# One tile for both heads' first 64 tokens in half of the attention units

## The chip, the cores and the metric

The kernel runs on one core of a Trainium2 chip. The metric is device time of one execution in microseconds, and of the kernel before three executions were timed. TensorE is called PE below, VectorE DVE, ScalarE ACT, GpSimd POOL, and the queue of SyncE that issues most DMAs SP.

## What is computed

Four batches of 8 heads, 576 tokens of 64 elements: causal attention plus a linear memory, mixed by a gate per head; then two feed-forward layers over the 2304 tokens (512 to 2048 to 512), all in float32.

```python
scores = np.where(causal, -1e9, scale * q @ k.T); scores -= scores.max(-1, keepdims=True)
a = np.exp(scores); a /= a.sum(-1, keepdims=True) + 1e-09
q_p = phi(q)                       # exp(min(q, 0)) + max(q, 0)
mem_out = (q_p @ M_prev) / (q_p @ z_prev + 1e-06)
x = g * mem_out + (1 - g) * (a @ v)
h = x @ w_in1;  x = (s * relu(h) ** 2 + b) @ w_out1
h = x @ w_in2;  x = (h * tanh(softplus(h))) @ w_out2
```

## The kernel before

**Attention units.** Function `pair` (L469) makes the steps of one unit: a batch, a pair of heads and a group of query tiles. Each head's 576 queries are padded with 64 rows of zeros in front, which gives five tiles of 128. A *leading* unit takes tiles 0 to 2, that is 320 tokens a head and 64 rows of padding in tile 0; a *trailing* unit takes tiles 3 and 4. There are 16 of each kind, 4 in each batch.

In a leading unit each head has its own tile `Pt` for t = 0, 1, 2, six in all, of 128 rows and 64 + (64 + 128 t) columns: the memory part and the keys up to the diagonal. The steps are: loads of q rows with z (`qn`, L514), of transposed q and k (`qk`, L521) and of M with v (`vx`, L656); phi(q), its product with z and the sums (L535 to L541) on POOL, ACT and DVE; six pairs of score matmuls (L571), the heads of a pair on the upper and lower 64 rows of PE; on DVE a minimum over `mask - scores` that leaves the masked scores in `Pt` (L581); the memory part scaled by `nm` on POOL (L592); the exponential on ACT with its row sum (L589); gate and reciprocal of the sums (L533, L610); the scaling by `rs` on POOL (L607, for batches 1 to 3); transposes on PE, twelve in a leading unit, eighteen in a trailing one (L630); copies out of PSUM on ACT (L635); the product with M and v (L652), for one block of keys after the other, both heads into one bank; a copy (L666) and a store to `x_d` (L668).

**Order of the work.** A planner (`Plan`, L193) writes the order of all engines' instructions down before the program is built. It plays the steps through with a cost, a priority and buffers for each, and what it gives is fixed: every engine takes its instructions in that order. Attention units have the lower number (50 + 7 per unit in batches 1 to 3, L1252) and go ahead of the first feed-forward layer (from 500, `RANK1`), whose matmuls (L881 into the hidden layer, L957 out of it) fill PE while attention waits for other engines. The rings of buffers are short: one of `qn`, `qk`, `vx` at first, two once the weights of layer 1 are converted (L1262), two of `PT`, `xs`, `ex` and of each `Pt`. Stores of the weights' sums and halves for the second layer (L825, L866, L868) go through SP at a late priority, between the loads of attention. At about 312 us attention ends, at about 485 us layer 2 begins (L1112 to L1188), which lasts to the end.

Of the kernel before, what the change touches and what calls it, by code (L numbers as in the profile page):

```python
# [9 lines left out]
F32 = mybir.dt.float32  # L10
F32R = mybir.dt.float32r
BF16 = mybir.dt.bfloat16
I32 = mybir.dt.int32
U32 = mybir.dt.uint32
AF = mybir.ActivationFunctionType
ALU = mybir.AluOpType
# [3 lines left out]
P = 128  # L20
MASKED = -1.0e30
HUGE = 3.0e38
TRUNC = -0.5 + 2.0 ** -13 - 2.0 ** -15
PE, ACT, DVE, POOL, DMA = range(5)
# [29 lines left out]
def act_us(n, extra=0):  # L54
    return 0.094 + 0.00083 * n + 0.093 * extra


def dve_us(n, fast=False):
    return 0.068 + (0.00052 if fast else 0.00104) * n


def pool_us(n):
    return 0.3 + 0.0013 * n
# [6 lines left out]
def two(s):  # L70

    s.two = True
    return s
# [119 lines left out]
class Plan:  # L193
# [29 lines left out]
    def add(self, engine, us, prio, f, r=(), w=(), after=(), keep=(), share=1.0):  # L223


        bufs = list({id(b): b for b in (*r, *w, *keep) if b.ring is not None}.values())
        new = [b for b in bufs if b.maker is None]
        waits = {id(s): s for b in r for s in b.writers}
        waits.update((id(s), s) for s in after)
        s = Step(engine, us, prio, f, list(waits.values()), bufs, new)  # L230
        s.share = share
        s.left = len(waits)
        for x in waits.values():
            x.next.append(s)
        for b in bufs:
            b.users += 1
            if b.maker is None:
                b.maker = s
            elif id(b.maker) not in waits:
                b.maker.next_start.append(s)  # L240
                s.left += 1
        for b in w:
            b.writers.append(s)
        self.steps.append(s)
        return s
# [114 lines left out]
def attention_then_two_ffn(ctx: ExitStack, tc: tile.TileContext, qk, qz, vm, beta,  # L360
# [3 lines left out]
    nc = tc.nc  # L364
    B, H = qk.shape[:2]
    NQ, D = qz.shape[3] - 1, qz.shape[4]
    SP = NQ * P
    S = SP - D
# [16 lines left out]
    SCALE = 1.0 / float(D) ** 0.5  # L385
    TA, TB = groups_all = tuple(range(3)), tuple(range(3, NQ))
    NONE = 5
    plan = Plan()
    add = plan.add
# [6 lines left out]
    ident = const.tile([P, P], F32, name="ident")  # L396
    make_identity(nc, ident)
    mask = const.tile([P, SP], BF16, name="mask")
# [3 lines left out]
    igate = const.tile([P, 2, H], F32, name="igate")  # L402
    sb = const.tile([P, 2], F32, name="sb")

    x_d = dram.tile([P, NCC, NT], F32, name="x_d")
# [9 lines left out]
    x_in = {(b, g): Buf() for b in range(B) for g in range(2)}  # L415
# [21 lines left out]
    small, att = ExitStack(), ExitStack()  # L437
    m1s = small.enter_context(tc.tile_pool(name="m1s", bufs=1))
    at = att.enter_context(tc.tile_pool(name="at", bufs=1, side="right"))
    m1t, m2a, m2c = [], [], []  # L440

    R = {}
# [22 lines left out]
    attention_steps = []  # L465
# [3 lines left out]
    def pair(b, p, prio, g, place=None, apart=False):  # L469
# [4 lines left out]
        def add(engine, us, f, r=(), w=(), keep=(), share=1.0):  # L474
            attention_steps.append(plan.add(engine, us, prio, f, r, w, keep=keep, share=share))
            return attention_steps[-1]
# [190 lines left out]
        c0 = b * S + q0  # L667
        add(DMA, 0.7, lambda: nc.sync.dma_start(x_d[:, p, c0:c0 + m], xs.t[:, :m]), [xs], [x_in[b, groups_all.index(g)]])  # L668


    W = {}

# [584 lines left out]
    n = len(plan.steps)  # L1257
# [3 lines left out]
    for x, a in zip(("qk", "qn", "vx"), (0, 832, 1344)):  # L1261
        R[x].homes(stage, [a], conversion_left)  # L1262
    for b, p, g, prio in halves_[H:]:
        pair(b, p, prio, g)
    R["c1"] = Ring("c1").homes(stage, [2048 + 256 * i for i in range(4)], conversion_left).more(m1s, 1, conversion_left)
    c1_steps = {"in": {r: [] for r in range(NR)}, "out": {r: [] for r in range(NR)}}
    for r in range(NR):
# [23 lines left out]
    order1, n = [], 0  # L1291
    for i in range(len(seq)):
        order1.append((i, True))
        for k in range(n, len(seq)):
# [3 lines left out]
            n = k + 1  # L1298
# [35 lines left out]
    n = len(plan.steps)  # L1334
# [26 lines left out]
    n = len(plan.steps)  # L1361
# [76 lines left out]
```

## Time and profile before

| | |
|---|---|
| median of 3 runs | 957.14 us (956.62 to 957.4) |
| the profiled execution | 956.4 us, of which its span 954.6 us |
| busy: PE, DVE, ACT, POOL | 98%, 81%, 67%, 23% of the span |
| mean granted PE clock | 0.999 |
| chain that ended last, by engine | PE 79%, DVE 4%, ACT 2%, DMA 1% |

The span runs from the first to the last instruction. Busy time of PE is that of matmuls in flight, so that short waits between matmuls don't show in it; the chain of waits gives starts, and from them the pace.

### The profile page before, as it was taken

To read this page: it belongs to the slowest core of one execution; us is meant where nothing else is said; L and a number is where in the kernel's file an instruction comes from. 1 tells how busy PE (TensorE), PEld (TensorE's weight loads), DVE (VectorE), ACT (ScalarE), POOL (GpSimd) and SP (SyncE) were. 2 spreads that over 40 slices of the span, in tenths; PEclk is the share of its full clock that TensorE was granted. 3 is DMA by queue.
4 is the path that set the end of the run, shared out by engine and by line. 5 is a ranking of instruction groups with operands and counts; after the bars stand their busy time and mean duration, and the time that the engine had idled before them with its cause. 6 is when DMAs were issued, how large, how long until landed. Compare 5 with 4: busy or idle time off the path is not lost.

```text
span 954.6 us, 19318 instructions
## 1 busy us (share of the span) xinstructions
PE 937.3 (98%) x6594; PEld 862.0 (90%) x6594; DVE 776.0 (81%) x1886; ACT 641.5 (67%) x1393; POOL 220.7 (23%) x377
## 2 busy tenths in 40 slices
PE   7899999999999999999999999999999999999998
PEld 6677788878788999888899999999999999999998
DVE  6999989899978787568658998889957799577874
ACT  6899878777777476889757865557634476344652
POOL 4635445577663000000023400000000000000000
PEclk9999999999999999999999999999999999999999
DMA  9976757999996789988885658885786655775545
GB/s 236 311 201 176 235 162 224 266 267 265 283 257 198 221 282 308 291 301 274 291 289 165 206 184 266 303 278 177 234 285 218 209 163 191 259 226 199 170 139 178
DMA packets 148339, 224.11 MB, mean 235 GB/s; under 512 B 15120, under 2 KB 122640, under 8 KB 141328
## 3 DMA queue, kind: packets, MB, share of 16 engines
q1 hardware_dynamic: 141408, 174.63, 59.4%
q0 software_dynamic: 6688, 48.24, 15.3%
q8 instruction: 52, 0.85, 0.4%
q14 instruction: 47, 0.39, 0.1%
q10 hardware_dynamic: 144, 0.00, 0.0%
HBM read 159.39 MB, written 63.44 MB: 233 GB/s over the span
## 4 chain that ended last, share of the span: by engine, by line
PE 79%; DVE 4%; ACT 2%; DMA 1%; issue 1%; POOL 0%; DVEq 0%; POOLq 0%
PE bank L1112 20%; PE bank L1185 19%; PE bank L881 12%; PE bank L957 12%; PE bank L1188 5%; PE bank L652 4%; PE bank L630 4%; PE bank L571 3%; DMA stage<-wi_sums_d 1%; DVE S L740 1%; DMA qn<-in_qz 0%; DVE g L1118 0%; DVE woh L740 0%; POOL Pt L607 0%; DVE g L1150 0%
## 5 line engine op out<-in xcount | busy, mean ns | idle before, releaser
L1112 PE MATMUL bank<-wi,woh 128*128 128x384 f32 x477 | 112.5, 334 | 0.0
L1112 PE MATMUL bank<-wi,wol 128*128 128x384 f32 x483 | 105.9, 335 | 0.8 <-DVE wil L1118 0.6
L1185 PE MATMUL bank<-wol,S 128*128 128x256 f32 x756 | 102.3, 283 | 0.0
L1185 PE MATMUL bank<-woh,S 128*128 128x256 f32 x756 | 101.9, 283 | 0.0
L1185 PEld LDWEIGHTS bank<-wol,S 128*128 128x128 f32 x756 | 96.2, 192 | 0.0
L1185 PEld LDWEIGHTS bank<-woh,S 128*128 128x128 f32 x756 | 95.9, 192 | 0.0
L1112 PEld LDWEIGHTS bank<-wi,wol 128*128 128x128 f32 x483 | 85.6, 188 | 1.6 <-DVE wil L1118 0.9
L1112 PEld LDWEIGHTS bank<-wi,woh 128*128 128x128 f32 x477 | 85.2, 188 | 0.4
L589 ACT ACTIVATE Pt<-Pt,mx 128x64 f32<-128x64 f32 (+4 forms) x152 | 82.6, 564 | 1.8 <-DVE mx L581 1.8
L635 ACT COPY PT<-bank 128x384 f32<-128x384 f32 (+2 forms) x160 | 68.2, 491 | 22.4 <-PE bank L630 15.0
L607 POOL TENSOR_SCALAR Pt<-Pt,rs 128x448 f32<-128x448 f32 (+3 forms) x100 | 65.7, 676 | 39.2 <-DVE rs L610 26.8
L592 POOL TENSOR_SCALAR Pt<-ex,nm 128x64 f32<-128x64 f32 x152 | 60.2, 419 | 63.1 <-DVE nm L541 35.4
L630 PE MATMUL bank<-ident,Pt 128*128 128x128 f32 x444 | 62.5, 275 | 6.1 <-DVE Pt L607 1.7
L630 PEld LDWEIGHTS bank<-ident,Pt 128*128 128x128 f32 x444 | 49.5, 140 | 11.2 <-issue 3.4
L581 DVE CUSTOM_DVE_ANT_0 Pt<-bank,mask 128x64 f32<-128x64 f32 (+3 forms) x152 | 50.5, 373 | 8.0 <-PE bank L571 5.7
L739 ACT CAST woh<-stage 128x1024 fp32r<-128x1024 f32 (+2 forms) x42 | 37.2, 885 | 27.4 <-PE bank L1112 17.9
L740 DVE TENSOR_TENSOR woh<-stage,woh 128x1024 fp32r<-128x1024 f32 (+2 forms) x42 | 42.7, 1018 | 13.8 <-ACT woh L739 13.7
L1125 POOL TENSOR_SCALAR woh<-woh,sb 128x384 f32<-128x384 f32 (+1 forms) x6 | 5.5, 916 | 183.3 <-ACT woh L1124 183.3
L739 ACT CAST S<-g 128x384 fp32r<-128x384 f32 x56 | 28.7, 513 | 27.2 <-PE bank L1185 19.2
L1092 POOL DMA_DIRECT2D woh<-wo_split_d x13 | 6.9, 530 | 156.2 <-DVE g L1150 76.4
L881 PE MATMUL bank<-xh,wi 128*128 128x256 f32 x256 | 42.5, 292 | 0.0
L957 PE MATMUL bank<-gl,woh 128*128 128x256 f32 x256 | 41.5, 288 | 0.0
(331 smaller groups left out, 2491.1 us busy)
## 6 DMA issues: line engine op xcount, KB each, us to landing
woh<-wo_split_d POOLq DMA_DIRECT2D x13, 1024.0 KB, 5.6
wol<-wi_split_d POOLq DMA_DIRECT2D x12, 1024.0 KB, 5.2
wol<-wo_split_d POOLq DMA_DIRECT2D x11, 1024.0 KB, 5.2
stage<-in_w_in SPq DMA_DIRECT2D x21, 512.0 KB, 5.6
stage<-in_w_out SPq DMA_DIRECT2D x19, 512.0 KB, 4.7
stage<-wi_d SPq DMA_DIRECT2D x24, 384.0 KB, 5.1
stage<-wo_d SPq DMA_DIRECT2D x18, 512.0 KB, 3.7
wo_split_d<-high SPq DMA_DIRECT2D x32, 256.0 KB, 4.6
```

Of the source, the lines that this page charges most:

```text
L581: nc.vector.tensor_tensor_reduce(at_t(i, t, D + lo, D + hi), x.t[:, a:a + hi - lo], mask[:, SP - w + lo:SP - w + hi], -SCALE, mx.t[:, i, t ...
L589: nc.scalar.activation(at_t(i, t, D, w + D), at_t(i, t, D, w + D), AF.Exp, bias=mx.t[:, i, t + k:t + k + 1], scale=-1.0, accum_out=rs.t[:, ...
L592: add(POOL, 0.33, lambda i=i, t=t: nc.gpsimd.tensor_scalar(at_t(i, t, 0, D), ex.t[:, i, t - lo_t, :], nm.t[:, i, t - lo_t:t - lo_t + 1], 1 ...
L607: (nc.vector if e == DVE else nc.gpsimd).tensor_scalar(x, x, r, *((None, ALU.mult) if e == DVE else (1.0, ALU.mult, ALU.mult)))
L630: nc.tensor.transpose(ps.t[:, x, :], at_t(i, t, c * P, (c + 1) * P), ident)
L635: (nc.vector.tensor_copy if dve else nc.scalar.copy)(PT[i].t[:, x:x + n], ps.t[:, :n])
L739: lambda: (nc.scalar.copy if e == ACT else nc.vector.tensor_copy)(t[0](0), src()), r, [t[2], half], after)
L740: lo = two(add(DVE, dve_us(n), prio, lambda: nc.vector.tensor_tensor(t[0](1), src(), t[0](0).bitcast(F32), op=ALU.subtract), [*r, half], [ ...
L881: nc.tensor.matmul(ph, w_at(nm, r, cc)[:, o:o + P], x_at(x, cc), start=(begin and part == 0 and cc == 0), stop=(part == 2 and cc == NCC - ...
L957: nc.tensor.matmul(acc[ec // per].t[:, (ec % per) * n:(ec % per + 1) * n], w_at(nm, fc // FPR, fc % FPR)[:, ec * P:(ec + 1) * P], t(x)[:, ...
L1112: nc.tensor.matmul(ps.t[:, :H2], w[i // 4].t[:, j, kk, at_], x[kk].t[:, k], start=begin and part == kk == 0, stop=part == 2 and kk == 1, s ...
L1185: nc.tensor.matmul(acc[t].t[:, :DH], s.t[:, j, t * P:(t + 1) * P], x.t[:, k, q % 4], start=q == part == 0, stop=q == NQ2 - 1 and part == 2)
```

## The change

Leading units of batches 1 to 3 (twelve of sixteen) are made by a new function `leading` in place of `pair`. Both heads' 64 tokens of tile 0 go into one tile from the minimum on, head 0 on rows 0 to 63 and head 1 on rows 64 to 127, so that a unit has five tiles instead of six. The score matmuls stay six, in pairs of equal width, with q taken at columns that put the tokens on the right rows. The gates are laid out for five tiles once at the start (`gates`), with the triangle for 64 tokens (`step_`). The load of q rows falls into four DMAs, the product with z into two instructions, and the product with M and v into four pairs of matmuls instead of three.

```diff
+    gates = at.tile([P, 2, H // 2, 5], F32, name="gates")
+    nc.vector.tensor_copy(gates[:, :, :, 1:].rearrange("p k a (h t) -> p (k a) h t", t=2),
+                          igate.rearrange("p k (a h) -> p (k a) h", h=2).unsqueeze(3).to_broadcast([P, H, 2, 2]))
+    step_ = at.tile([P, D], BF16, name="step")
+    for i in range(2):
+        x = slice(D * i, D * i + D)
+        nc.vector.tensor_copy(gates[x, :, :, 0], igate[x, :, i::2])
+        nc.gpsimd.tensor_copy(step_[x], mask[x, SP - P + D * i:SP - P + D * i + D])
...
+    def leading(b, p, prio):
...
+        n_q, n_k, n_s = 320, 384, 5
+        widths = 64, 192, 320, 192, 320
...
+        add(DMA, 0.5, lambda: nc.sync.dma_start(zq(4, 4).rearrange("p (h t) d -> p h t d", t=2), qz[b, hs, :, 2:4].rearrange("h p a d -> p h a d")), w=[q_in])
+        for i in range(2):
+            add(DMA, 0.15, lambda i=i: nc.sync.dma_start(q_in.t[rows(i), 2 * D:4 * D].rearrange("p (s d) -> p s d", d=D), qz[b, 2 * p + i, D:, 0:2]), w=[q_in])
+        add(DMA, 0.25, lambda: nc.sync.dma_start(zq(0, 2), qz[b, hs, :, 0].rearrange("h p d -> p h d")), w=[q_in])
...
+            def weigh(a=a, n=n):
+                x, y, z = zq(3 + a, n), ex.t[:, a:a + n], zq(2, 1)
+                if a:
+                    x, y = (u.rearrange("p (h t) d -> p h t d", t=2) for u in (x, y))
+                    z = zq(0, 2).unsqueeze(2).to_broadcast([P, 2, 2, D])
+                nc.vector.tensor_tensor(x, y, z, op=ALU.mult)
+
+            two(add(DVE, dve_us(n * D), weigh, [ex, q_in], [q_in]))
...
+        where = [(0, 0, 0), (0, 0, D), (1, 0, 0), (0, 1, D), (1, 1, 0)]
+        for x, us, mine in ((0, 256, (0, 1)), (1, 320, (2,))):
+            def mm(x=x, mine=mine):
+                for t in mine:
+                    for i in range(2):
+                        q0 = P * t if t else D - D * i
+                        o, w = (D if t == 1 else 0), widths[t]
+                        nc.tensor.matmul(sc[x][i].t[:, o:o + w], qk_in.t[rows(i), q0:q0 + P], qk_in.t[rows(i), n_k:n_k + w], start=True, stop=True)
+
+            add(PE, 0.03 + us * 0.00167, mm, [qk_in], sc[x], [*(Pt if x == 0 else ()), mx, rs], 1.0)
...
+        for s in (0, 1, 3, 2, 4):
+            w, (x, k, a) = widths[s], where[s]
+
+            if s == 0:
+                for i in range(2):
+                    add(DVE, 0.14 + 0.00105 * w, lambda i=i: nc.vector.tensor_tensor_reduce(
+                        Pt[0].t[rows(i), D:P], sc[0][i].t[rows(i), :D], step_[rows(i)], -SCALE, HUGE, ALU.add, ALU.min, mx.t[rows(i), 0:1]),
+                        [sc[0][i]], [Pt_in[0], mx_in[0]], [Pt[0], mx])
+            else:
...
+        for x, o, blocks in ((0, 0, [(0, 0), (1, 0), (1, 1)]), (1, 0, [(3, 0), (3, 1)]),
+                             (0, 3, [(2, c) for c in range(3)]), (1, 2, [(4, c) for c in range(3)])):
...
+            for c, k in ((0, 0), (0, 1), (1, 1), (2, 1)):
+                for i in range(2):
+                    y = pv.t[rows(i)]
+                    if k == 0:
+                        dest, src = y[:, :D], PT[0].t[:, 0, rows(i)]
+                    elif c < 2:
+                        dest, src = y[:, D:n_q].rearrange("p (t q) -> p t q", t=2), PT[i].t[:, 1 - i + c:4 - i + c:2]
+                    else:
+                        dest, src = y[:, 192:n_q], PT[i].t[:, 5 - i]
+                    nc.tensor.matmul(dest, v_in.t.rearrange("p (h t d) -> p h t d", h=2, d=D)[:, i, c], src,
+                                     start=k == 0, stop=k == 0 or c == 2, skip_group_check=k > 0)
...
     for b, p, g, prio in halves_[H:]:
-        pair(b, p, prio, g)
+        if g == TA:
+            leading(b, p, prio)
+        else:
+            pair(b, p, prio, g)
```

In the built programs PE's last 3133 instructions, those of layer 2, stand in the same order before and after. Up to there the planner moves much. In the order of PE before, the last product of attention stands behind 896 of the 1920 matmuls of layer 1; in that of the change it stands behind 740. Between the scores of one leading unit and those of the next, in the last five intervals before, stand 36, 52, 48, 44 and 44 matmuls of layer 1; in the last six of the change 28, 28, 28, 28, 28 and 32. Score and product matmuls use half of PE's array each; the places where a full-array matmul follows one of them number 40 before and 38 after. From the load of q rows of one leading unit to that of the next, SP has 117 issues in the last five intervals of the change.

PE, the transposes of one leading unit, before (L630 is the transpose, L881 and L957 are matmuls of layer 1):

```order
L630 MATMUL bank_120<-ident,Pt_0_2354 128x128
L630 MATMUL bank_120<-ident,Pt_0_2356 128x128 x2
L881 MATMUL bank_119<-xh_1625,wih_0_1713 128x256 x4
L630 MATMUL bank_124<-ident,Pt_1_2355 128x128
L630 MATMUL bank_124<-ident,Pt_1_2357 128x128 x2
L630 MATMUL bank_126<-ident,Pt_0_2358 128x128 x3
L881 MATMUL bank_119<-xh_1625,wil_0_1722 128x256 x4
L630 MATMUL bank_125<-ident,Pt_1_2359 128x128 x3
```

And in the change, late in attention (L778 is the new transpose, L1090 is what L957 was):

```order
L778 MATMUL bank_125<-ident,Pt_0_3282 128x128
L778 MATMUL bank_125<-ident,Pt_0_3283 128x128 x2
L778 MATMUL bank_123<-ident,Pt_1_3285 128x128 x2
L1090 MATMUL bank_121<-gh_2834,woh_0_2011 128x256 x2
L1090 MATMUL bank_122<-gh_2834,woh_0_2011 128x256 x2
L778 MATMUL bank_126<-ident,Pt_0_3284 128x128 x3
L1090 MATMUL bank_121<-gh_2834,wol_0_2025 128x256 x2
L1090 MATMUL bank_122<-gh_2834,wol_0_2025 128x256 x2
L778 MATMUL bank_120<-ident,Pt_1_3286 128x128 x3
```

One transpose is gone, the groups are 3, 2, 3 and 3 instead of four of 3, and layer 1's matmuls still stand between the groups.

PE, the product with M and v of one leading unit, before and then in the change (64 is the output's rows of a head, the second number its columns):

```order
L652 MATMUL bank_125<-PT_2568,vx_2400 64x384
L652 MATMUL bank_125<-PT_2581,vx_2400 64x384
L652 MATMUL bank_125<-PT_2568,vx_2400 64x256
L652 MATMUL bank_125<-PT_2581,vx_2400 64x256
L652 MATMUL bank_125<-PT_2568,vx_2400 64x128
L652 MATMUL bank_125<-PT_2581,vx_2400 64x128
```

```order
L795 MATMUL bank_120<-PT_3446,vx_3329 64x64 x2
L795 MATMUL bank_120<-PT_3446,vx_3329 64x256
L795 MATMUL bank_120<-PT_3452,vx_3329 64x256
L795 MATMUL bank_120<-PT_3446,vx_3329 64x256
L795 MATMUL bank_120<-PT_3452,vx_3329 64x256
L795 MATMUL bank_120<-PT_3446,vx_3329 64x128
L795 MATMUL bank_120<-PT_3452,vx_3329 64x128
```

The first pair of 384 columns has become one of 64 and one of 256.

SP, the loads of the first leading unit of batch 1, before and then in the change (L702 and L835 load weights):

```order
L702 DMA stage<-in_w_out 128x1024
L656 DMA wil_0_689<-in_vm 128x2x320
L514 DMA qn_775<-in_qz 128x2x256
L521 DMA qk_796<-in_qk 64x2x384 x2
L656 DMA vx_814<-in_vm 128x2x192
```

```order
L664 DMA wil_0_696<-in_vm 128x2x320
L699 DMA qn_782<-in_qz 128x2x128
L701 DMA qn_782<-in_qz 64x128 x2
L702 DMA qn_782<-in_qz 128x2x64
L704 DMA qk_813<-in_qk 64x2x384 x2
L798 DMA vx_833<-in_vm 128x2x192
```

One issue has become four, so that the loads of `qk` and `vx` stand three issues later.

## Rows read from the trace of the kernel before

**Rows 1.** The page: span, and busy time of each engine.

```profile
span 954.6 us, 19318 instructions
...
PE 937.3 (98%) x6594; PEld 862.0 (90%) x6594; DVE 776.0 (81%) x1886; ACT 641.5 (67%) x1393; POOL 220.7 (23%) x377
```

**Rows 2.** Busy time by stretch: PE, PEld, DVE, ACT, POOL, PE clock, DMA share, GB/s.

```profile
200.00:220.00 20.00, 20.00 (x171) 16.61 (x169) 18.48 (x62) 16.37 (x47) 16.48 (x28) 1.00 0.91 257
...
500.00:520.00 20.00, 19.18 (x110) 18.54 (x109) 17.33 (x33) 15.71 (x29) 8.19 (x8) 1.00 0.52 153
540.00:560.00 20.00, 19.16 (x109) 18.55 (x108) 20.00 (x36) 15.02 (x28) 1.88 (x1) 1.00 0.37 124
```

**Rows 3.** The chain of waits, 20 to 320 us: start, length, what.

```profile
204.96 1.29 PE bank L571 x12
206.25 1.45 PE bank L652 x12
207.69 0.67 PE bank L881 x4
208.37 1.96 PE bank L630 x18
210.80 2.03 PE bank L571 x12
212.84 2.10 PE bank L652 x20
214.93 0.67 PE bank L881 x4
215.60 0.48 PE bank L957 x4
...
219.78 1.29 PE bank L571 x12
```

**Rows 4.** Waits of PE, 60 to 320 us: in total, times, longest.

```profile
PE bank L630 <- POOL Pt L607: 1.7, 2, 1.3
PE bank L630 <- ACT PT L635: 0.8, 1, 0.8
PE bank L630 <- DVE nm L533: 0.4, 1, 0.4
```

**Rows 5.** Groups by line and shape, 130 to 310 us: busy us, mean ns, idle before.

```profile
L592 POOL TENSOR_SCALAR Pt<-ex,nm 128x64 f32<-128x64 f32 x100 | 36.7, 390 | 35.2 <-DVE nm L541 20.3 <-PE bank L571 5.9 <-DVE nm L533 3.9
...
L607 POOL TENSOR_SCALAR Pt<-Pt,rs 128x64 f32<-128x64 f32 x20 | 9.7, 500 | 18.0 <-DVE rs L610 14.2 <-ACT Pt L589 2.8 <-ACT xs L666 1.0
...
L581 DVE CUSTOM_DVE_ANT_0 Pt<-bank,mask 128x64 f32<-128x64 f32 x38 | 7.5, 217 | 3.3 <-PE bank L571 3.1 <-POOL Pt L592 0.2
...
L589 ACT ACTIVATE Pt<-Pt,mx 128x64 f32<-128x64 f32 x20 | 7.2, 382 | 0.0
...
L538 DVE TENSOR_TENSOR stage<-ex,stage 128x384 f32<-128x384 f32 x8 | 4.4, 551 | 0.1
```

**Rows 6.** DVE in order of time at the start: start, length, what, idle before.

```profile
7.08 0.17 DVE L430 TENSOR_SCALAR igate<-igate 128x16 f32<-128x16 f32 x1 [0.28 <-ACT igate L429]
8.18 0.69 DVE L717 SCALAR_TENSOR_TENSOR stage<-stage 128x512 int32<-128x512 int32 x1 [0.93 <-ACT stage L713]
```

**Rows 7.** SP issuing DMAs in order of time: start, length, what, count.

```profile
197.08 0.44 SPq L514 DMA_DIRECT2D stage<-in_qz  x1
...
198.12 0.46 SPq L517 DMA_DIRECT2D qn<-in_qz  x1
...
209.66 1.39 SPq L521 DMA_DIRECT2D qk<-in_qk  x2
...
212.28 0.38 SPq L514 DMA_DIRECT2D stage<-in_qz  x1
```

**Rows 8.** DMA issues: KB each, median us from issue to landing.

```profile
qk<-in_qk SPq DMA_DIRECT2D x24, 192.0 KB, 4.0
...
stage<-in_qz SPq DMA_DIRECT2D x8, 256.0 KB, 4.4
```

More of the change, by code (lines that the diff above doesn't have):

```diff
@@ L668, in pair, with add, rows, zq @@
         add(DMA, 0.7, lambda: nc.sync.dma_start(x_d[:, p, c0:c0 + m], xs.t[:, :m]), [xs], [x_in[b, groups_all.index(g)]])
+    def leading(b, p, prio):
+        def add(engine, us, f, r=(), w=(), keep=(), share=1.0):
+            attention_steps.append(plan.add(engine, us, prio, f, r, w, keep=keep, share=share))
+            return attention_steps[-1]
+        hs = slice(2 * p, 2 * p + 2)
+        n_q, n_k, n_s = 320, 384, 5
+        widths = 64, 192, 320, 192, 320
+        qk_in, q_in, v_in = Buf(R["qk"], [P, 2 * n_k]), Buf(R["qn"], [P, 8 * D]), Buf(R["vx"], [P, 6 * D])
+        def rows(i):
+            return slice(D * i, D * i + D)
+        def zq(a, n):
+            return q_in.t[:, a * D:(a + n) * D].rearrange("p (s d) -> p s d", d=D)
+        def q_all():
+            return zq(3, 5)
+        add(DMA, 0.5, lambda: nc.sync.dma_start(zq(4, 4).rearrange("p (h t) d -> p h t d", t=2), qz[b, hs, :, 2:4].rearrange("h p a d -> p h a d")), w=[q_in])
[3 more added lines that the diff above has]
+        for i in range(2):
+            add(DMA, 0.0009 * 2 * n_k, lambda i=i: nc.sync.dma_start(
+                qk_in.t[rows(i)].rearrange("p (a n) -> p a n", a=2),
+                qk[b, 2 * p + i, rows(i)].rearrange("p (a n) -> p a n", a=2)[:, :, :n_k]), w=[qk_in])
+        ex = Buf(R["ex"], [P, n_s, D])
+        nm, mx, rs = (Buf(R[x], [P, 16]) for x in ("nm", "mx", "rs"))
+        n_e = n_s * D
+        def gate(x, k, eps):
+            nc.vector.scalar_tensor_tensor(x, x, eps, gates[:, k, p], op0=ALU.add, op1=ALU.mult)
+        add(POOL, 0.3 + 0.0032 * n_e, lambda: nc.gpsimd.tensor_scalar_min(ex.t, q_all(), 0.0), [q_in], [ex])
+        add(ACT, act_us(n_e), lambda: nc.scalar.activation(ex.t, ex.t, AF.Exp), [ex], [ex])
+        two(add(DVE, dve_us(n_e), lambda: nc.vector.scalar_tensor_tensor(ex.t, q_all(), 0.0, ex.t, op0=ALU.max, op1=ALU.add), [ex, q_in], [ex]))
+        for a, n in ((0, 1), (1, 4)):
+            def weigh(a=a, n=n):
[5 more added lines that the diff above has]
+            two(add(DVE, dve_us(n * D), weigh, [ex, q_in], [q_in]))
+        add(DVE, dve_us(n_e), lambda: nc.vector.tensor_reduce(nm.t[:, :n_s], q_all(), axis=mybir.AxisListType.X, op=ALU.add), [q_in], [nm])
+        add(DVE, 0.15, lambda: gate(nm.t[:, :n_s], 0, 1e-6), [nm], [nm])
+        add(DVE, 0.09, lambda: nc.vector.reciprocal(nm.t[:, :n_s], nm.t[:, :n_s]), [nm], [nm])
+        Pt = [Buf(R["Pt0"], [P, P]), *(Buf(R[f"Pt{t}"], [P, P * (t + 1)]) for _ in range(2) for t in (1, 2))]
+        Pt_in, mx_in, rs_in = ([Buf() for _ in widths] for _ in range(3))
+        sc = [[Buf(R["a"], [P, 512]) for _ in range(2)] for _ in range(2)]
+        where = [(0, 0, 0), (0, 0, D), (1, 0, 0), (0, 1, D), (1, 1, 0)]
[7 more added lines that the diff above has]
+            add(PE, 0.03 + us * 0.00167, mm, [qk_in], sc[x], [*(Pt if x == 0 else ()), mx, rs], 1.0)
+            attention_steps[-1].mode = 1
+        for s in (0, 1, 3, 2, 4):
[6 more added lines that the diff above has]
+            else:
+                add(DVE, 0.14 + 0.00105 * w, lambda s=s, w=w, x=x, k=k, a=a: nc.vector.tensor_tensor_reduce(
+                    Pt[s].t[:, D:D + w], sc[x][k].t[:, a:a + w], mask[:, SP - w:], -SCALE, HUGE, ALU.add, ALU.min, mx.t[:, s:s + 1]),
+                    [sc[x][k]], [Pt_in[s], mx_in[s]], [Pt[s], mx])
+            add(POOL, 0.33, lambda s=s: nc.gpsimd.tensor_scalar(Pt[s].t[:, :D], ex.t[:, s], nm.t[:, s:s + 1], 1.0, op0=ALU.mult, op1=ALU.mult),
+                [ex, nm], [Pt_in[s]], [Pt[s]])
+            add(ACT, 0.28 + 0.00083 * w, lambda s=s, w=w: nc.scalar.activation(
+                Pt[s].t[:, D:D + w], Pt[s].t[:, D:D + w], AF.Exp, bias=mx.t[:, s:s + 1], scale=-1.0, accum_out=rs.t[:, s:s + 1]),
+                [Pt_in[s], mx_in[s]], [Pt_in[s], rs_in[s]], [Pt[s], mx, rs])
+        gated, done = Buf(), Buf()
+        add(DVE, 0.15, lambda: gate(rs.t[:, :n_s], 1, 1e-9), rs_in, [gated], [rs])
+        add(DVE, 0.09, lambda: nc.vector.reciprocal(rs.t[:, :n_s], rs.t[:, :n_s]), [gated], [done], [rs])
+        for s in (0, 1, 3, 2, 4):
+            w = widths[s]
+            add(POOL, pool_us(w), lambda s=s, w=w: nc.gpsimd.tensor_scalar(
+                Pt[s].t[:, D:D + w], Pt[s].t[:, D:D + w], rs.t[:, s:s + 1], 1.0, ALU.mult, ALU.mult), [done, Pt_in[s]], [Pt_in[s]], [Pt[s], rs])
+        PT = [Buf(R["PT"], [P, 9, P]) for _ in range(2)]
+        for x, o, blocks in ((0, 0, [(0, 0), (1, 0), (1, 1)]), (1, 0, [(3, 0), (3, 1)]),
+                             (0, 3, [(2, c) for c in range(3)]), (1, 2, [(4, c) for c in range(3)])):
+            ps, n = Buf(R["a"], [P, 4, P]), len(blocks)
+            def turn(ps=ps, blocks=blocks):
+                for y, (s, c) in enumerate(blocks):
+                    nc.tensor.transpose(ps.t[:, y], Pt[s].t[:, c * P:c * P + P], ident)
+            add(PE, 0.01 + 0.109 * n, turn, [Pt_in[s] for s in sorted({s for s, _ in blocks})], [ps], [PT[x], *(Pt[s] for s, _ in blocks)])
+            add(ACT, act_us(n * P) - 0.04, lambda x=x, o=o, n=n, ps=ps: nc.scalar.copy(PT[x].t[:, o:o + n], ps.t[:, :n]), [ps], [PT[x]])
+        pv, xs = Buf(R["a"], [P, 512]), Buf(R["xs"], [P, 320])
+        def mm():
+            for c, k in ((0, 0), (0, 1), (1, 1), (2, 1)):
+                for i in range(2):
+                    y = pv.t[rows(i)]
[7 more added lines that the diff above has]
+                                     start=k == 0, stop=k == 0 or c == 2, skip_group_check=k > 0)
+        add(DMA, 0.75, lambda: nc.sync.dma_start(v_in.t.rearrange("p (h t d) -> p h t d", h=2, d=D), vm[b, hs, :, :3].rearrange("h p a d -> p h a d")), w=[v_in])
+        add(PE, 0.04 + 704 * 0.00167, mm, PT + [v_in], [pv])
+        attention_steps[-1].mode = 2
+        add(ACT, act_us(n_q) - 0.04, lambda: nc.scalar.copy(xs.t, pv.t[:, :n_q]), [pv], [xs])
+        add(DMA, 0.7, lambda: nc.sync.dma_start(x_d[:, p, b * S:b * S + n_q], xs.t), [xs], [x_in[b, 0]])
```

## Prediction

> **What bounds the kernel now.** I read the page first: PE is busy for 937.3 of 954.6 us, and the next engine, DVE, for 776.0 [rows 1]. A mean over stages with different limits is no proof, so I read the busy time by stretch. While attention and layer 1 share the engines, at 200 to 220 us, PE is busy for all of 20.00 us, DVE for 18.48, ACT for 16.37 and POOL for 16.48 [rows 2]. Then the chain of waits, because it says what ends last there: from 204.96 us on it is PE alone, scores, product, layer 1, transposes, scores, each starting where the one before ends [rows 3]. So in this stretch a microsecond of PE work is a microsecond of time, and work of DVE, ACT or POOL costs nothing as long as PE finds its data ready. Last the waits of PE: from 60 to 320 us they come to 1.7 + 0.8 + 0.4 = 2.9 us, all ahead of transposes [rows 4]. At the start of layer 2, around 510 and 550 us, PE lacks 20.00 - 19.18 and 20.00 - 19.16, together 1.66 us, beside a DVE that is busy for 20.00 [rows 2]. I leave these as they are: PE's order is the same there, and so is the work on the other engines.
>
> **The sum, on PE.** Twelve units change.
>
> *Transposes.* Eighteen take 1.96 us [rows 3], 0.109 us each. One a unit goes: -0.109.
>
> *Scores.* The same six matmuls, with the same widths: 0.
>
> *Product with M and v.* A leading unit streams 384 + 256 + 128 = 768 columns a head in 1.45 us; a trailing one 4 x 256 + 128 = 1152 in 2.10 [rows 3]. The difference gives 0.65 / 384 = 1.69 ns a column, with 1.45 - 768 x 1.69 ns = 0.15 us beside. Now 64 + 256 + 256 + 128 = 704 columns: -64 x 1.69 ns = -0.108. Against that stand two more instructions, a pair with only 64 columns. The trace of before has no such product, so I bound it. Below: nothing, if it costs its columns alone, as the slope between the two units says of wider ones. Above: what 64-column matmuls cost in the scores. Those stream 64 + 192 + 320 = 576 columns in 1.29 us and 64 + 448 + 512 = 1024 in 2.03 [rows 3], which is 1.65 ns a column and 0.34 us beside, 0.19 more than the product has. I put all of that on the 64-column pair. Score matmuls hold 128 columns of weights and these 64, and both streams keep the heads side by side, so the nearer row is the product's own: I take 0.05. The product saves 0.06 (bounds: saves 0.108, costs 0.08).
>
> The Trainium skill speaks against this split: TensorEngine Tiling (Array Packing), Instruction Overhead, says that a matmul carries some 60 cycles of overhead on trn2, that one with a single column takes as long as one with 60, and that a dimension which is small already should not be cut further. No run here shows such a split yet. Worked out from that figure as an estimate, four more passes (the trace shows two records for each instruction) of 60 cycles at 2.4 GHz are 0.10 us; the product would then save 0.01, and the whole sum would be 1.8 us instead of 2.4.
>
> Together 0.109 + 0.06 = 0.17 us a unit, 2.0 us for twelve (bounds 0.3 and 2.6).
>
> *Returns to the full array.* Four layer-1 matmuls take 0.67 us right behind a product and 0.48 elsewhere [rows 3], so each return costs 0.19. There are 40 before and 38 after: -0.4 us.
>
> That makes 2.4 us less PE work.
>
> **What lies beside PE.** A unit loses one memory scaling and one scaling by the sum on POOL (0.390 + 0.500 us), and one exponential on ACT (0.382 with its row sum's read-out behind it) [rows 5]. The minimum over 64 tokens stays two instructions, and half the partitions don't shorten the 0.217 us [rows 5]. On DVE the product with z becomes two instructions for 320 columns in place of one for 384 that takes 0.551 [rows 5], about even. I count all of it at nothing: PE's chain covers it. If the cover failed, it would appear as a wait ahead of the transposes, the only place where PE waits now.
>
> *The start.* Three short copies on DVE and two on POOL are new. The nearest row is the add on the gates, 0.17 us, and DVE then idles for 0.93 us until its first conversion [rows 6]: 3 x 0.17 = 0.51 fits. POOL idles there too. Cost 0; if they did not fit, 0.1 to 0.2.
>
> *The order.* With less to do a unit, the planner puts leading units 28 layer-1 matmuls apart instead of about 44. Nothing is saved by that, since layer 1's matmuls only move behind attention: one interval of PE work shrinks from 44 x 0.12 + 30 x 0.109 + 1.29 + 1.45 + 2.03 + 2.10 + 0.38 = 15.8 us to 28 x 0.12 + 29 x 0.109 + 6.8 + 0.38 = 13.7 us, and the matmuls left over come later. But every other queue must do an interval's work in 13.7 us, which leads to the rivals.
>
> **Forecast.** The profiled execution took 956.4 us, so it would be 954.0; it lies 0.7 under the median of the runs, and from the median the time is 957.14 - 2.4 = 954.7 us. Waits of PE stay as they are in sum. A measurement of this kernel can tell some 0.2% from no change, here 1.9 us: faster is below 955.2, slower above 959.1.
>
> **Rivals.**
>
> *SP falls behind, and PE waits for loads (slower).* From the load of q rows at 197.08 us to that of the next leading unit at 212.28, SP issues 23 DMAs, one per 0.66 us [rows 7]. In the change an interval has 117 / 5 = 23.4 issues. At 0.66 they take 15.4 us, 1.7 more than PE's 13.7. At the 0.44 and 0.46 of the loads of q rows themselves [rows 7] they take 10.5 and nothing is late. So SP loses 0 to 1.7 us an interval, 0 to 12 us over seven. The loads have a lead to lose first: those of `qk` issue at 209.66 within 1.39 us, the second after about 0.7, land 4.0 later [rows 7, 8] at some 214.4, and the scores start at 219.78 [rows 3], 5.4 us later. At the full loss PE waits 12 - 5.4 = 6.6 us and the time is 961.3. It is above 957.14 when an interval loses over (5.4 + 2.4) / 7 = 1.1 us, and above 959.1 from 1.4. For it: 0.66 us an issue may well be all that SP can do, and the load of q rows, which lands after 4.4 us now [rows 8], gets three issues more. Against it: the new DMAs are small, and of the 23.4 issues only 9.4 are not attention's own, where before it were 12 of 23. Chance 0.17.
>
> *The small product eats the gain (no difference).* With the 64-column pair at its upper bound and the rest as above, 0.3 + 0.4 = 0.7 us are left: 956.4. For it: 0.19 us is what 64-column scores show. Chance 0.22.
>
> *The waits ahead of transposes go as well (faster still).* 1.7 us wait on POOL and 0.8 on ACT [rows 4]; both engines lose work in these units. All gone: 954.7 - 2.5 = 952.2. Against it: the planner has already spent the lighter load on a tighter order, so the slack is not left over. Chance 0.13.
>
> *The change doesn't do what it says.* The built order has 11 transposes a unit and five tiles; I give this nothing.
>
> **How the numbers follow.** The forecast has the remaining 0.48. The range reaches down to the third rival with 0.3 us of measurement, 951.9, and up into the first, 960.0; outside are the worst of the first rival and luck below, 0.1 each. Faster by over 0.2%: three quarters of the forecast (0.36; the rest has the product nearer its upper bound), nearly all of the third rival (0.12) and a little of the second: 0.50. Slower: most of the first rival (0.13) and some disorder that I have not seen: 0.16. No difference: 0.34.
>
> **What would show it.** Right: 132 transposes in place of 144 in these units, the product of a leading unit at 1.38 to 1.40 us in the chain, returns at 0.67, PE's waits between 60 and 320 us still near 3 us, layer 2 beginning about 2.4 us earlier, attention ending some 20 us earlier. Wrong: a product at 1.45 or more (second rival); PE waiting ahead of scores or products, or DMA landings of `qk`, `vx` or q rows in its chain (first rival); waits below 1 us (third). A change in layer 2's length would be something that none of these explains.

## Result and profile after

The change made the kernel slower: 964.46 us median of six runs (962.09 to 966.33) against 957.27 (956.44 to 957.67), a ratio of 1.0075 with a 95% interval of 1.0057 to 1.0092. Forecast were 954.7 us and a range up to 960.0. The profiled execution took 964.18 us, of which its span is 962.4.

The page and the busy time by stretch (columns as in [rows 2]) of the change:

```profile
span 962.4 us, 19439 instructions
...
PE 939.5 (98%) x6630; PEld 863.9 (90%) x6630; DVE 775.3 (81%) x1901; ACT 635.4 (66%) x1369; POOL 205.8 (21%) x355
```

```profile
100.00:120.00 20.00, 18.23 (x136) 16.02 (x137) 20.00 (x54) 16.76 (x38) 10.12 (x13) 0.91 0.80 249
160.00:180.00 20.00, 17.63 (x148) 15.49 (x146) 16.68 (x55) 13.22 (x35) 13.37 (x24) 1.00 0.88 229
...
260.00:280.00 20.00, 18.59 (x157) 14.02 (x156) 15.56 (x55) 13.35 (x38) 11.65 (x21) 1.00 0.91 250
500.00:520.00 20.00, 19.40 (x112) 19.08 (x111) 15.65 (x29) 15.30 (x28) 7.85 (x8) 1.00 0.58 171
540.00:560.00 20.00, 19.39 (x110) 18.78 (x109) 20.00 (x38) 16.73 (x34) 6.37 (x6) 1.00 0.53 181
```

Layer 2 lacks no more than before ([rows 2], last two); the loss lies ahead of it. PE lacks 20.00 - 17.63 = 2.37 us at 160 to 180 and 20.00 - 18.59 = 1.41 at 260 to 280, and DVE, ACT and POOL are all busy for less there than before at 200 to 220 [rows 2]. The waits of PE from 60 to 320 us, which were 2.9 us and all ahead of transposes [rows 4]:

```profile
PE bank L1014 <- DVE rt L1072: 2.0, 2, 1.8
PE bank L579 <- DMA stage<-in_qk: 1.2, 1, 1.2
PE bank L778 <- POOL Pt L768: 1.1, 4, 0.4
PE bank L638 <- POOL Pt L615: 0.9, 1, 0.9
PE bank L638 <- ACT PT L643: 0.8, 1, 0.8
PE bank L638 <- DVE mx L754: 0.6, 1, 0.6
PE bank L741 <- DMA qk<-in_qk: 0.4, 1, 0.4
PE bank L795 <- ACT PT L781: 0.2, 1, 0.2
```

They come to 7.2 us, and scores now wait for loads. The engine named is often only the last link; the chain of waits of the change, late in attention (start, length, what), goes further back:

```profile
221.89 0.42 SPq L699
...
222.36 0.48 SPq L701
...
222.88 2.75 DMA stage<-in_qz
...
225.81 1.01 POOL ex L715
226.82 1.59 POOL Pt L768 x3
...
228.45 0.44 PE bank L778 x2
...
230.28 6.18 DMA stage<-in_qk
...
237.03 4.01 DMA stage<-in_qz
...
247.46 1.35 PE bank L795 x16
248.81 0.67 PE bank L1090 x4
...
264.05 4.03 DMA stage<-in_qk
...
268.21 2.07 PE bank L579 x8
```

Where the chain of before is PE alone [rows 3], this one runs through SP and loads. A load of q rows lands at 225.63; only then does POOL take up that unit's phi(q) (L715), and the scalings (L768), which stand behind it in POOL's order, release the transposes at 228.45. SP itself in that stretch (start, length, what, count):

```profile
219.49 0.40 SPq L664 DMA_DIRECT2D stage<-in_vm  x1
220.00 0.45 SPq L676 DMA_DIRECT2D x_d<-xs  x1
220.79 0.99 SPq L999 DMA_DIRECT2D wi_resident_d<-wi  x2
221.89 0.42 SPq L699 DMA_DIRECT2D stage<-in_qz  x1
222.36 1.12 SPq L701 DMA_DIRECT2D stage<-in_qz  x2
223.52 0.59 SPq L702 DMA_DIRECT2D stage<-in_qz  x1
224.21 1.21 SPq L704 DMA_DIRECT2D qk<-in_qk  x2
225.46 0.59 SPq L999 DMA_DIRECT2D wi_resident_d<-wi  x1
```

Each row begins 0.04 to 0.11 us behind the one before, but for one pause of 0.34. A row joins issues of one line and hides the pauses between them, so I give the sums here issue by issue, from the starts and ends in the trace. Over 200 to 280 us SP issues for 70.4 of 80 us in the change (124 issues, 0.57 us each on average), and its pauses of over 0.2 us come to 1.0; the rest are shorter gaps. Before, it issued for 67.3 us (118 issues), with 4.8 of pauses. The 0.59 us an issue and the 70.6 us in the expectations below are read from joined rows and are a little too high.

So two theories stood at first. **Theory 1:** SP has no time for its issues, three more in each of twelve leading units, 666 instead of 630 in all. **Theory 2:** the order is too tight for the engines beside PE, and SP's count is innocent.

### The profile page after: what moved, and what is told of

Its sections match the earlier page's. It is cut to its first block, busy times and chain, and to the rows that moved or that the text cites. A ratio compares the mean times of both kernels' runs of the same rounds, so it can differ in the third digit from the quotient of the medians.

```text
span 962.4 us, 19439 instructions
## 1 busy us (share of the span) xinstructions
PE 939.5 (98%) x6630; PEld 863.9 (90%) x6630; DVE 775.3 (81%) x1901; ACT 635.4 (66%) x1369; POOL 205.8 (21%) x355
## 4 chain that ended last, share of the span: by engine, by line
PE 70%; DMA 3%; DVE 2%; ACT 1%; issue 1%; POOL 1%; SPq 0%; DVEq 0%; POOLq 0%
PE bank L1245 23%; PE bank L1318 18%; PE bank L1090 11%; PE bank L1014 10%; PE bank L1321 5%; DMA stage<-in_qk 1%; DMA woh<-wi_split_d 1%; PE bank L660 1%; DMA stage<-in_qz 1%; PE bank L579 1%; PE bank L638 1%; PE bank L778 1%; PE bank L795 0%; DVE S L873 0%; POOL Pt L768 0%
## 5 line engine op out<-in xcount | busy, mean ns | idle before, releaser
L643 ACT COPY PT<-bank 128x384 f32<-128x384 f32 (+2 forms) x112 | 46.3, 496 | 9.8 <-PE bank L638 9.2
L597 ACT ACTIVATE Pt<-Pt,mx 128x448 f32<-128x448 f32 (+4 forms) x80 | 50.8, 641 | 2.6 <-DVE mx L589 1.8
L638 PE MATMUL bank<-ident,Pt 128*128 128x128 f32 x300 | 40.3, 277 | 6.6 <-DVE Pt L615 2.4
L638 PEld LDWEIGHTS bank<-ident,Pt 128*128 128x128 f32 x300 | 32.8, 141 | 11.9 <-issue 3.5
L1090 PE MATMUL bank<-gh,woh 128*128 128x256 f32 x256 | 41.8, 287 | 0.0
L1090 PE MATMUL bank<-gl,woh 128*128 128x256 f32 x256 | 41.5, 287 | 0.0
L1090 PE MATMUL bank<-gh,wol 128*128 128x256 f32 x256 | 41.2, 286 | 0.0
L600 POOL TENSOR_SCALAR Pt<-ex,nm 128x64 f32<-128x64 f32 x80 | 33.1, 434 | 33.5 <-DVE nm L549 16.0
```

The lines of the kernel that those rows point to most:

```text
L597: nc.scalar.activation(at_t(i, t, D, w + D), at_t(i, t, D, w + D), AF.Exp, bias=mx.t[:, i, t + k:t + k + 1], scale=-1.0, accum_out=rs.t[:, ...
L600: add(POOL, 0.33, lambda i=i, t=t: nc.gpsimd.tensor_scalar(at_t(i, t, 0, D), ex.t[:, i, t - lo_t, :], nm.t[:, i, t - lo_t:t - lo_t + 1], 1 ...
L638: nc.tensor.transpose(ps.t[:, x, :], at_t(i, t, c * P, (c + 1) * P), ident)
L643: (nc.vector.tensor_copy if dve else nc.scalar.copy)(PT[i].t[:, x:x + n], ps.t[:, :n])
L1090: nc.tensor.matmul(acc[ec // per].t[:, (ec % per) * n:(ec % per + 1) * n], w_at(nm, fc // FPR, fc % FPR)[:, ec * P:(ec + 1) * P], t(x)[:, ...
```

## Experiments

All are compared with the kernel before on the same chip, where it took 957.6 to 958.1 us; small differences between chips are therefore better read from the ratios. Times are medians.

### Issues without order, order without issues

The kernel before with its load of q rows in four issues, in its own order:

```diff
-            add(DMA, 1.0, lambda: nc.sync.dma_start(part(qn_b, 1, n_t + 1), qz[b, hs, :, :n_t + 1]...), w=[qn_b])
+                nc.sync.dma_start(dst[:, :, 2:4], src[:, :, 2:4])
+                for i in range(2):
+                    nc.sync.dma_start(dst[D * i:D * i + D, 1, 0:2], src[D * i:D * i + D, 1, 0:2])
+                nc.sync.dma_start(dst[:, 0, 0:2], src[:, 0, 0:2])
```

> The kernel before, whose load of q rows in the twelve leading units of batches 1 to 3 is cut into four issues of the same bytes; everything else, the order too, stays. Theory 1 (SP is too slow for its issues): an interval of 15.8 us then holds 26 issues instead of 23; at the 0.59 us that an issue takes in the change's trace that is 15.3 us and just fits, at 0.66 it is 17.2, so I expect 958 to 962 us, with loads in the chain of waits. Theory 2 (the order is too tight for the engines beside PE, SP's count is innocent): 957 us, within 0.2%.

Measured: 966.8 us, ratio 1.0097 (1.0082 to 1.0113), more than either theory said. Its trace was taken in a run of its own:

> The kernel before with q rows in four issues once more, for its trace. Theory 1: between 200 and 280 us SP issues without a pause (before 70.6 of 80 us), and loads of q rows, of q and k or of M and v end waits of PE that total some 8 us between 160 and 320 us. Theory 3: SP has pauses, and only the loads of q rows are late.

963.83 us once; SP issues for 69.6 of 80 us with 2.1 of pauses, and PE's waits are 6.2 us from 60 to 320, not quite the 8 expected. 36 issues alone, in the order of before, cost as much as the whole change.

The change with one issue in place of its four, in its own order:

```diff
-        add(DMA, 0.5, lambda: nc.sync.dma_start(zq(4, 4)..., qz[b, hs, :, 2:4]...), w=[q_in])
+        add(DMA, 0.5, lambda: nc.sync.dma_start(q_in.t..., qz[b, hs, :, 0:4]...), w=[q_in])
+        for i in range(2):
+            add(DMA, 0.15, lambda: None, w=[q_in])
+        add(DMA, 0.25, lambda: None, w=[q_in])
```

> The change, whose q rows of a leading unit come by one issue of the same size as before's, so that tile 0 holds rows that don't belong there (the output of these units is not computed rightly); order and all other instructions stay. Theory 1: an interval has 20.4 issues, 12.0 us at 0.59, less than PE's 13.7; the waits from 160 to 300 us (about 9 us in the change's profile against 1.3 before) go for the most part, 955 to 958 us. Theory 2: the tight order stays, so do the waits: 963 to 965 us.

Measured: 956.43 us, ratio 0.9984 (0.9973 to 0.9995). PE's waits of this run:

```profile
PE bank L1014 <- DVE rt L1072: 2.0, 2, 1.8
PE bank L638 <- ACT PT L643: 0.7, 1, 0.7
PE bank L741 <- DMA qk<-in_qk: 0.6, 2, 0.3
PE bank L778 <- POOL Pt L768: 0.3, 1, 0.3
```

The order is the change's, and 8.0 us of loss are gone. Theory 2 falls here. Tile 0 holds wrong rows in this run; the runs further down with whole output and two or three issues take no longer. The next two look at the order by itself, the planner's least cost of an issue being raised:

```diff
-                    end, got.done = max(now + 0.45, dma - BACKLOG), dma + 1.6 + got.lag
+                    end, got.done = max(now + 0.6, dma - BACKLOG), dma + 1.6 + got.lag
```

> The change, planned with at least 0.60 us for each issue of SP instead of 0.45; the same instructions in another order (attention ends behind 804 matmuls of layer 1 instead of 740, 36 to 44 matmuls an interval late in attention instead of 28). Theory 1: the loads get their time in the plan, some 957 us, and SP no longer behind. Theory 2: the order is looser by about half of what it was tightened, so about half of the loss goes: 960 us.

> The kernel before, planned with 0.60 us for each issue: its own work in an order as tight as the change's (attention ends behind 748 matmuls, about 32 an interval late in attention, so 14.3 us of PE work), with 18 to 24 issues an interval, 20.4 on average. Theory 1: 20.4 issues at 0.59 are 12.0 us and fit, so 957 us, within 0.4%. Theory 2: a tight order alone costs what it cost the change, 961 to 965 us.

Measured: 958.54 us for the change (1.0002 to 1.0023), between what the two theories said; 957.86 for the kernel before in a tight order (0.9991 to 1.0010), as theory 1 said. The first still has all its 666 issues, in an order that leaves SP 4.6 us of pauses at 200 to 280. The planner had reckoned with 0.45 us at least for an issue that takes 0.57 on average.

### Which issues: any, or these loads?

**Theory 3** was left: the cut loads themselves come late, and SP's time is not the point. So 36 stores of weights were cut instead, which nothing in attention waits for:

```diff
-                            nc.sync.dma_start(WIR[r][:, o, x, :, slot].bitcast(F32), src(i, j)[:, o])
+                            for k in ((0, 1), (1, 2)) if r < 3 else ((0, 2),):
+                                nc.sync.dma_start(WIR[r][:, o, x, k[0]:k[1], slot].bitcast(F32), src(i, j)[:, o, k[0]:k[1]])
```

> The kernel before, with 36 stores of layer 1's weights for layer 2 (between 164 and 276 us) each cut into two issues of the same rows and the same packets; the loads of attention and the order stay. Theory 1 (SP's time is what is short, whatever it issues): 36 issues at 0.59 us are 21 us more of SP work in that stretch, as in the run with cut q loads, so 962 to 968 us. Theory 3 (the cut loads themselves are late, because four small ones land later than one or because small packets burden the DMA engines): these loads are whole here, so 957 us, within 0.2%.

Measured: 969.19 us, ratio 1.0116 (1.0101 to 1.0131), more than either theory said. The stores delay what stands behind them on SP, and PE waits at the end of that:

```profile
PE bank L630 <- POOL Pt L607: 4.6, 3, 3.1
PE bank L652 <- ACT PT L635: 2.3, 1, 2.3
PE bank L630 <- DVE nm L533: 1.4, 1, 1.4
```

Theory 3 falls: loads that were whole cost nothing less. The landing times speak against it too: the 64-row loads of the change land in 3.7 us, the single big one of the run with one issue in 5.8 (issues of both: KB each, median us to landing):

```profile
stage<-in_qz SPq DMA_DIRECT2D x16, 32.0 KB, 3.7
```

```profile
stage<-in_qz SPq DMA_DIRECT2D x8, 256.0 KB, 5.8
```

The opposite, 36 stores taken from SP and issued by POOL (`nc.gpsimd if r < 3 else nc.sync`):

> The change as it is, its four loads included, but 36 stores of layer 1's weights are issued by POOL and no longer by SP; order, bytes and packets stay. Theory 1: SP has 630 issues, so the loss of 8 us goes and 956 to 959 us remain, as far as POOL's issues (some 0.53 us each on an engine that is busy for 60% there) don't delay its scalings. Theory 3 (the small loads themselves): 964 us.

Measured: 965.2 us (1.0058 to 1.0091), no gain. SP had its pauses (15.5 of 80 us), but POOL's issue takes longer than I had put down (group by line, 130 to 310 us: busy us, mean ns, idle before):

```profile
L999 POOL DMA_DIRECT2D wi_resident_d<-wi x24 | 18.2, 760 | 0.0
```

36 x 0.76 = 27 us on POOL made its scalings late: PE waits 2.5 + 2.2 us for L615 and L768, where it was 0.9 + 1.1 in the change. The run shows neither theory right; it moved the bottleneck.

### How much SP can take

Here the host lays q, z and the packed rows out as the tile wants them, so that the output is whole at any number of issues; the order stays the change's.

```diff
+        "qp": np.concatenate(parts, axis=3),
...
+        for us, lo, hi in ((0.5, 0, 4), (0.15, 4, 6), (0.15, 6, 8), (0.25, 0, 0)):
+            add(DMA, us, (lambda lo=lo, hi=hi: nc.sync.dma_start(q_in.t[:, D * lo:D * hi], qp[b, p][:, D * lo:D * hi])) if hi else (lambda: None), w=[q_in])
```

> The change in its own order, with the rows of a leading unit laid out by the host and brought by two issues of equal size: 642 issues of SP in all, where one gives 630 (956.4 us in a run before this) and four give 666 (964.5). If SP has reserve up to some count and none beyond it: 956.5 to 957.5 us. If each issue costs alike, 8 us for 36 issues: 956.4 + 12 x 0.22 = 959.1.

> The same with three issues, 654 in all. With a reserve that ends: 958.5 to 960.5 us, most of the loss falls to the last twelve issues or the twelve before. Alike: 956.4 + 24 x 0.22 = 961.7.

> The change in its own order, rows laid out by the host and brought by four issues of 128 whole rows of 512 bytes: 666 issues, as many as in the change. Theory 1 with a reserve (SP loses its last pauses near 654 issues, then every issue costs its 0.5 to 0.6 us): 962 to 965 us. Theory 4 (the loads on 64 rows and the 256-byte pieces are what costs): 957 us, as with three such issues (956.6).

> The same with five issues, 678. Theory 1 with a reserve: 12 more issues cost 12 x 0.5 = 6 us more than four, 968 to 971 us. Theory 4: 957 to 958 us.

The change's own loads, the two of 64 rows as one (**theory 4:** their kind is what costs):

> The change with its own loads of tiles 1 and 2 and of z (the 256-byte pieces stay), but one load of 128 rows in place of the two of 64: 654 issues. Theory 1 with a reserve: 957 us, within 0.2% of the run with three issues (956.6). Theory 4: about half of the loss, 960 us, or all of it, 964, if the pieces of z are to blame.

And the kernel before with half of those stores cut (`if r < 3 and o == 0`):

> The kernel before with 18 stores of layer 1's weights, each second one of the 36, cut into two issues: 648 in all. Theory 1 with a reserve as in the change: 957 to 959 us, where 36 cost 11.6 us. Alike for each issue: 963 us.

SP's time for the q rows of one leading unit is the number of issues by their median duration, from the trace of each run (minimum, median, maximum in ns; eight of the twelve units load into `stage`). The change, then one, two, three, four and five issues, then the mixed ones:

```profile
L701 SPq DMA_DIRECT2D stage<-in_qz x16: 477/576/611, 161.4 to 269.8; - x16
L699 SPq DMA_DIRECT2D stage<-in_qz x8: 403/444/850, 160.9 to 267.1; - x8
L702 SPq DMA_DIRECT2D stage<-in_qz x8: 373/586/1131, 162.6 to 270.4; - x8
```

```profile
L699 SPq DMA_DIRECT2D stage<-in_qz x8: 373/436/837, 159.2 to 255.9; - x8
```

```profile
L700 SPq DMA_DIRECT2D stage<-in_qp x16: 346/451/2737, 160.7 to 259.4; - x16
```

```profile
L700 SPq DMA_DIRECT2D stage<-in_qp x24: 400/480/1432, 161.0 to 263.7; - x24
```

```profile
L700 SPq DMA_DIRECT2D stage<-in_qp x32: 328/430/1097, 160.8 to 270.0; - x32
```

```profile
L700 SPq DMA_DIRECT2D stage<-in_qp x40: 328/423/1239, 160.3 to 269.7; - x40
```

```profile
L699 SPq DMA_DIRECT2D stage<-in_qz x8: 403/522/1428, 161.2 to 262.2; - x8
L700 SPq DMA_DIRECT2D stage<-in_qp x8: 345/480/1386, 161.7 to 263.2; - x8
L702 SPq DMA_DIRECT2D stage<-in_qz x8: 432/441/547, 162.2 to 265.2; - x8
```

A median leaves out the few issues of 1 to 2.7 us that each run has, so the table also gives the sum over the twelve units, and for the kernel before what the stores of L866 (L867 where they are cut) take in all. Pauses are those of over 0.2 us between single issues, in the one execution that was profiled.

| order, run | issues in all | SP a unit, us (medians) | SP in all for these loads or stores, us | pauses of SP, 200 to 280 us | time, us | ratio (95%) |
|---|---|---|---|---|---|---|
| change, one | 630 | 0.44 | 5.5 | 10.3 | 956.43 | 0.9984 (0.9973 to 0.9995) |
| change, two | 642 | 0.90 | 13.7 | 3.4 | 956.01 | 0.9980 (0.9968 to 0.9992) |
| change, three | 654 | 1.44 | 18.0 | 3.8 | 956.62 | 0.9985 (0.9972 to 0.9997) |
| change, mixed | 654 | 1.44 | 18.9 | 2.9 | 957.76 | 1.0000 (0.9988 to 1.0012) |
| change, four | 666 | 1.72 | 24.0 | 1.1 | 961.25 | 1.0041 (1.0023 to 1.0058) |
| the change | 666 | 2.18 | 25.9 | 1.0 | 964.46 | 1.0075 (1.0057 to 1.0092) |
| change, five | 678 | 2.12 | 26.4 | 1.3 | 966.99 | 1.0090 (1.0070 to 1.0111) |
| before | 630 | | 26.5 | 4.8 | 957.3 | |
| before, 18 stores cut | 648 | | 35.0 | 1.1 | 963.67 | 1.0062 (1.0044 to 1.0081) |
| before, 36 stores cut | 666 | | 40.5 | 2.8 | 969.19 | 1.0116 (1.0101 to 1.0131) |

This is a reserve that ends, a little later than I had expected of two and three issues; four and five came out 1 us under what I expected. With 2.9 us of pauses or more in those 80, the time stays at 956 to 958.5; with 2.8 or less it is 961 and more. That border is narrow, and beyond it the pauses don't order the runs: the 36 cut stores leave 2.8 us and cost most. Within each order SP's time does. From three issues to four, to the change's four and to five, SP has 5.9, 7.9 and 8.4 us more, and the time grows by 4.6, 7.8 and 10.4, so behind the knee a microsecond of SP is about one of time (0.8 to 1.2). The change's loads are dearer than equal ones (25.9 against 24.0 us for four), which is what is left of theory 4: the kind counts by the time that SP needs for it. For the kernel before I had expected the same reserve, and that was wrong: 18 issues add 8.5 us of SP there and cost 6.0 at once, 36 add 14.0, not the 21 of the expectation, and cost 11.6. That is a reserve of some 2.5 us and then one for one. It fits the pauses, 4.8 us before and 10.3 in the change with one issue; more than this fit is not shown.

### A version without the loss

> The change with q, z and the packed rows of a leading unit laid out by the host as the tile wants them, so that one issue brings what four brought, and planned so; the output is whole. Theory 1: as many issues as before (630), attention ends behind 828 matmuls of layer 1; the loss goes and the saving on PE shows, 954.5 to 957 us. Theory 2 (the order) would say about 960, since the order lies between those of before and of the change.

> The same, planned with 0.60 us for each issue: another order, tighter (attention ends behind 772 matmuls). Theory 1: 630 issues fit here too, 954 to 957 us; what is left to gain or lose is the wait of layer 1 on DVE at about 113 us with the half clock behind it, some 3 us in the change's profile, which no theory of SP touches. Theory 2: over 960.

Host-laid rows in one issue, planned so: 955.63 us, ratio 0.9977 (0.9968 to 0.9987). Planned with 0.60 us an issue: 957.08 (0.9984 to 1.0001), at the edge of its range: nothing is gained by the other order. Then q and k of both heads in one issue as well:

```diff
-        "qk": np.concatenate([np.concatenate([qt, qt], axis=2), np.concatenate([kt, kt], axis=2)], axis=3),
+        "qk": np.concatenate([qt, kt], axis=3).reshape(nb, nh // 2, 2 * nd, -1),
```

> The change with host-laid rows in one issue and, in the same order as that run, q and k of both heads in one issue too: 598 issues in all. Theory 1: SP already has pauses at 630 issues, so there is nothing more to gain: 955.0 to 956.0 us. If each issue cost alike, 32 fewer would give 7 us more: 948.6.

> The change with both loads laid out, planned with one step for q and k: an order a little tighter (attention ends behind 808 matmuls instead of 828). Theory 1: SP has pauses in either order, so 953.5 to 955.5 us.

> The kernel before, in its own order, with q and k of both heads laid out by the host for one issue: 598 issues, as many as in the run of the change with both loads laid out (954.17 us). If the sum on PE is right (2.4 us), 956.6 us here; if the change saves nothing on PE, 954.2. If SP cost the kernel before nothing, it stays within 0.2% of 957.6 in any case.

Measured: 954.17 us (0.9963, 0.9948 to 0.9977) and, replanned, 954.61 (0.9961, 0.9946 to 0.9975); both beat the kernel before and the change. The first came out 0.8 us under its range, so there may have been something left to gain with 10.0 us of pauses (0.9963 against 0.9977, with intervals that overlap). The kernel before with the same relief takes 956.46 (0.9984, 0.9974 to 0.9994): the relief gains 1.4 us there too. With 19.3 and 16.8 us of pauses of SP, the change is worth 956.46 - 954.17 = 2.3 us. The two were measured on different chips; by their ratios it is 2.0 us, and with both intervals 0.3 to 3.7.

## Why the prediction was wrong

- **The sum on PE fits:** 2.4 us forecast, 2.3 measured between the two relieved kernels, though with a wide interval, and with 2.3 and 2.9 us of listed waits of PE in their profiles. Transposes: one less in each unit. Product: 1.35 us at 247.46 in the chain, and in all twelve units, instead of 1.45 [rows 3], so it saves 0.10 and not 0.06; the small pair costs its columns and little else, the lower bound. With 0.10 the sum is 2.9. The Trainium skill's figure for overhead (TensorEngine Tiling (Array Packing), Instruction Overhead), added to each matmul as the prediction did, would have it save 0.01; the trace does not agree with that reading. The return to the full array takes 0.67 at 248.81, as forecast.
- **The start was right, the work beside PE only in its sum.** The copies take 0.53 us of DVE's pause of 0.93 [rows 6], and the first conversion begins at 8.14 us, not later than before. With both loads laid out PE's waits come to 2.3 us, less than the 2.9 of before, but they are others: 0.8 us ahead of transposes and 1.5 of layer 1 on DVE, which the kernel before did not have and the prediction did not name.
- **The step that failed is "Waits of PE stay as they are in sum".** Its sum has no term for SP's time, and that term decided. The waits rose from 2.9 to 7.2 us in the view of waits, layer 2 starts at 474.66 us instead of 467.73, where 2.4 earlier was forecast, and with one issue in place of four the same order takes 956.43 us. Short gaps that this view doesn't list make up part of the rest; I have not divided them up.
- **The first rival was the one, and it was priced too low in three places.** Its lower end, 0.44 and 0.46 us an issue, came from loads that are cheaper to issue than the new ones (0.576 and 0.586); that they are small in bytes was no argument, since the issue of 32 KB takes longer than one of 256 KB (0.436 in the run with one issue). Its 5.4 us between landing and use were counted as a lead that has to be lost first; the cut stores show only some 2.5 us, as 18 of them cost 6.0. The lead was read on `qk`, while the chain at 221.89 to 228.45 runs through the load of q rows. And seven intervals were counted, though PE already lacks 2.4 us at 160 to 180. So the full price of 961.3 was too low, and the range ended below the result. One outcome says little of a chance of 0.17, but the pauses, which spoke for more, were left out of it.
- **What I had in hand and did not read:** I took SP's pace from one interval (23 issues in 15.2 us) and asked whether it could be faster. Adding up its pauses would have shown 4.8 us in 80, with three more issues for each of five units in that stretch to come, by my estimate 3 x 5 x 0.55 = 8 us. The Trainium skill (Perfetto Trace Analysis, What "DMA-bound" means) names an issuing track that is solid with DMA issues as a bound of its own; this trace agrees, with 70.4 of 80 us issuing and 1.0 of pauses.
- The other rivals: the small product did not eat the gain. The waits ahead of transposes did not go in the change (1.1 + 0.9 + 0.8 + 0.6 us in the list above); with SP relieved they fell to 0.8, and the wait on DVE took most of their place.

## To carry to other kernels

Count a queue that issues DMAs like an engine: its issues by their durations from the trace, whatever their bytes, and above all its pauses in the stretch that is bound elsewhere. As long as it has pauses more issues cost little (up to 654 in this change's order), and behind that each costs about its whole time, also stores that nothing nearby waits for. If a new layout needs more pieces, have them laid out ahead so that one issue brings them, and give a planner the issue time that the trace shows.

## What was not expected of the hardware

- The issues of one line on SP take 0.34 to 0.59 us by their median in the change (lines with at least four, 130 to 310 us), not by their bytes, and single ones up to 2.5. One of the stores on POOL takes 0.76 on average, so moving issues there is no way out when POOL has work that others wait for.
- The change's order and the replanned one of the kernel before have a wait of layer 1 on DVE (L1072, there L939) near 114 us, and the clock behind it is not always the same. PE in order of time, in the change and then with one issue:

```profile
115.80 1.86 PE L1014 MATMUL bank<-xh,wi 128*128 128x256 f32 x8 [1.77 <-DVE rt L1072]
117.46 1.05 PE L1090 MATMUL bank<-gh,woh 128*128 128x256 f32 x4
```

```profile
116.08 1.21 PE L1014 MATMUL bank<-xh,wi 128*128 128x256 f32 x8 [1.77 <-DVE rt L1072]
117.13 0.64 PE L1090 MATMUL bank<-gh,woh 128*128 128x256 f32 x4
```

Eight matmuls take 117.46 - 115.80 = 1.66 us in the change and 117.13 - 116.08 = 1.05 with one issue. The granted clock over 100 to 120 us is 0.91 in the change, so the lower of its two levels (1.2 GHz) for part of it, and 1.00 with one issue. Why it falls in one run and not in the other stays open. The wait is in both runs and so no part of the 8 us. The lower clock costs the profiled execution of the change 1.5 us there (4.00 us against 2.49 for the first twenty matmuls), but over a whole execution the mean granted clock is 0.993 to 0.998 in the change and 0.994 to 0.998 with one issue, so it does not tell the two kernels apart.
